# Block 2's attention with keys in token layout and queries turned by VectorE

## The chip, the core and the metric

The kernel runs on one core of a Trainium2 chip. A core has five engines that each work through a queue of their own in order: TensorE (PE in the profile; its weight loads are listed apart as PEld), VectorE (DVE), ScalarE (ACT), GpSimd (POOL) and SyncE (SP), whose queue here issues nearly all DMA transfers. An instruction that waits for a semaphore holds up everything behind it on its own engine. The metric is the device time of one execution in microseconds (us); lower is better.

## What is computed

```python
# q, k, v: (8 batches, 8 heads, 576 tokens, 64) f32
q_s = exp(q - max(q, axis=-1));  q_s = q_s / (sum(q_s, axis=-1) + 1e-9)   # over the 64 of a head
k_s = exp(k - max(k, axis=2));   k_s = k_s / (sum(k_s, axis=2) + 1e-9)    # over the 576 tokens
kv  = einsum('bhsd,bhse->bhde', k_s, v)                                   # 64x64 per head
x   = einsum('bhsd,bhde->bhse', q_s, kv)       # then heads side by side: 4608 tokens x 512
h   = x @ w_in                                 # 512 -> 2048, weights given in float64
g   = h * clip(h + 3, 0, 6) / 6
out = g @ w_out                                # 2048 -> 512
```

## The kernel before

The 4608 tokens are worked off in six pieces: blocks 0, 1 and 2 of 512 tokens each, by a plain matrix product, and then three large blocks of 1024 tokens each, by a product with seven instead of eight sub-products (functions `factors`, `phase1`, `phase2`). The attention of a piece is made while the piece ahead of it is multiplied. So block 2's attention, which the change rewrites, is made in the loop `j == 1`, beside block 1's matrix products, and the first large block's attention in the loop `j == 2`.

Loop j goes over 16 chunks of 128 hidden units; I call them f0 to f15. In a chunk TensorE does 12 matmuls `ph <- x, w` (the first product, `gemm1`), ScalarE and VectorE make `g` from `ph` (`relu6`) and split it into two parts `gp` (a ScalarE cast, then a VectorE subtraction on line 121), and TensorE does 12 matmuls `po <- w, gp` (the second product, `gemm2`). The second product of a chunk comes behind the first product of the next one (`pend`, one chunk of lag). Both parts of every operand are used, three matmuls for one product, to keep float32 accuracy. Beside this each chunk of block 1 makes sums of weights for the large blocks (`sum_weights`: VectorE additions `v <- w` and `v <- v`, splits `gp <- v`, and DMA stores `wf <- gp`). Tile `gp` has four buffers, which the splits of `g` and of the sums share.

The attention of a block is four units, one for each pair of heads (`hp`). Each unit is a generator, and `steps` advances it by a step or two per chunk. A unit of block 2 before, `attention(2, hp)`, runs so:

- loads `kt` (keys with channels on the partitions, 128x576), `qt` (queries with tokens on the partitions, 128x512) and `vt` (values);
- `km`, a VectorE maximum over `kt`, then a ScalarE exponential of `kt`; `q_softmax` with `lean`: a VectorE maximum `qm`, eight ScalarE exponentials that also give the sums `qr`, then VectorE normalizes `qt`;
- on TensorE, five turnings of `kt` into tiles `pe` and `pe2` and four of `qt` into `tp` (`flip`, line 93), which ScalarE copies to `ke` (keys with tokens on the partitions) and `qT`;
- ten pairs of small matmuls `pkv <- vt, ke`, whose result VectorE scales to `kv`; the matmuls `px <- qT, kv`; and a split of `px` into block 2's `x`.

A unit of a large block, `sb_attention(s, hp)`, goes another way: it loads the keys twice, `kt` for the maximum only and `ke` in token layout; the maximum is spread by GpSimd to a 128x128 tile `kb`, which TensorE turns with one flip into `pm`; VectorE subtracts it from `ke`, and ScalarE takes the exponential. Its queries come in a layout `qf` in which every 32x32 block is already standing the wrong way, so that VectorE's own 32x32 transposes give `qT` (in tile `m`). A head's 64 channels then lie on two groups of 32 partitions, so the maximum and the sum have to be combined across partitions: `both_halves` lets GpSimd copy 32 partitions at a time into `swap`, and VectorE combines (line 304).

What sets the order: a scheduler places the instructions of VectorE, ScalarE, GpSimd and SP at build time. On TensorE, from block 1 on, the order is that of the program (`keep_in_program_order`). `kt` and `qt` have one buffer each, `ke` and `vt` two, `km` and `kb` two.

Of the kernel before, what the change touches and what calls it, by code (L numbers as in the profile page):

```python
# [18 lines left out]
P = 128  # L19
# [13 lines left out]
def attention_moe(  # L33
# [51 lines left out]
    def mm(out, lhsT, rhs, start, stop, goes_on=False):  # L85
        ordered(
            nc.tensor.matmul(  # L87
                out, lhsT, rhs, start=start, stop=stop, skip_group_check=goes_on
            )
        )  # L90
# [199 lines left out]

    NG = SB // QD
    START = NB * TB

    def across(t):
        return t.rearrange("p (g o) -> p g o", o=1).broadcast_to([P, NG, QD])

    def both_halves(stat, op):
        swap = att.tile([P, NG], F32, name="swap", bufs=2)  # L300
        for r in range(0, P, QD):
            o = r ^ QD
            nc.gpsimd.tensor_copy(swap[r : r + QD], stat[o : o + QD])  # L303
        nc.vector.tensor_tensor(stat, stat, swap, op=op)

    def q_softmax_t(qt):
        qs = qt.rearrange("p (g d) -> p g d", d=QD)
        qm = att.tile([P, NG], F32, name="qm", bufs=2)
        qr = att.tile([P, NG], F32, name="qr", bufs=2)
# [4 lines left out]
        nc.vector.tensor_reduce(qr, qs, axis=AX.X, op=ALU.add)  # L314
# [4 lines left out]
        qT = moe.tile([P, 2 * DM], F32, name="m", bufs=1)[:, 0:SB]  # L319
        nc.vector.transpose(qT, qt)  # L320
        return qT

# [2 lines left out]
    def x_of(s):  # L325

        if "x" not in held:
            held["x"] = xp.tile([P, NCC, SB], F32, name="x32", tag="xa")
        return held["x"]

    def sb_attention(s, hp):
        t0 = START + s * SB
        need = [b for b in range(t0 // S, (t0 + SB - 1) // S + 1)]
        qt = att.tile([P, SB], F32, name="qt", bufs=1)
        nc.sync.dma_start(qt, qf[s, hp])
        loads = {b: load_k(b, hp, tokens=True) for b in need if (b, hp) not in kvs}
        yield
        new = {}
        for b, (kt, ke, vt) in loads.items():
            km = att.tile([P, 1], F32, name="km", bufs=2)  # L340
            nc.vector.tensor_reduce(km, kt, axis=AX.X, op=ALU.max)
            kb = att.tile([P, P], F32, name="kb", bufs=2)
            nc.gpsimd.tensor_copy(kb, km.broadcast_to([P, P]))
            new[b] = ke, vt, kb
        qT = q_softmax_t(qt)
        yield
        for ke, vt, kb in new.values():
            pm = bank_a("pm")
            flip(pm[:, 0:P], kb)
            nc.vector.tensor_sub(  # L350
                ke, ke, pm[:, 0:P].rearrange("p (o n) -> p o n", o=1).broadcast_to([P, NCH, P])
            )
            nc.scalar.activation(ke, ke, AF.Exp)
        yield
        yield
        for b, (ke, vt, kb) in new.items():
            kv_of(b, hp, ke, vt)
        yield
        x = x_of(s)
        for c in range(2):  # L360
            px = bank_a("px")
            at = t0 + c * TH
            for b in need:
                lo, hi = max(b * S - at, 0), min((b + 1) * S - at, TH)
                if lo < hi:
                    sl = slice(c * TH + lo, c * TH + hi)
                    mm(px[:, lo:hi], kvs[b, hp], qT[:, sl], True, True)
            nc.scalar.copy(x[:, hp, c * TH : (c + 1) * TH], px[:, 0:TH])
        yield


    A11, A12, A22, S1, S2, S3, S4 = range(7)
# [333 lines left out]
    def steps(units, length):  # L706
        before = None
        for unit in units:
            next(unit)
            yield  # L710
            if before:
                next(before, None)
            for _ in range(length - 2):
                next(unit)
                yield
            before = unit
        yield
        next(before, None)
        yield
# [19 lines left out]
    for j in range(NB):  # L739
        if j == 1:  # L740
            in_order.append(True)
        if j < NB - 1:
            step = steps([attention(j + 1, hp) for hp in range(NP)], 4)
        else:
            step = steps([sb_attention(0, hp) for hp in (0, 2, 1, 3)], 6)
            fac = factors(0)
        chunks = [*range(NFC)] if j < NB - 1 else [NFC - 1, *range(NFC - 1)]
        for n, f in enumerate(chunks):
            if not j and f + AHEAD < NFC:
                load_w(f + AHEAD)  # L750
            g = gemm1(j, f)
            if not j and f + 2 < NFC:
                decode(f + 2)
            if j == 1 and f % 2:
                plain_weights(f // 2, 0)
                plain_weights(f // 2, 1)
            if j:
# [19 lines left out]

    for s in range(NS):
        more = s + 1 < NS
        step = steps([sb_attention(s + 1, hp) for hp in (0, 2, 1, 3)], 6) if more else iter(())  # L780
# [12 lines left out]
        phase1(s, between1)  # L793
        phase2(s, between2)
        for _ in fac:
            pass
# [5 lines left out]
def _laid_out(q, k, v, moe_w_in, moe_w_out):  # L802
# [4 lines left out]
    n_first = _OUTS[0][0][0]  # L807
# [10 lines left out]
    if w.dtype != np.float64:  # L818
# [1 line left out]
    return {  # L820
        "q": tokens.transpose(0, 3, 2, 1, 4, 5),
        "qf": rows[n_first:]
        .reshape(-1, SB // QD, QD, NP, 4, QD)
        .transpose(0, 3, 4, 2, 1, 5)
        .reshape(-1, NP, P, SB),
        "kT": k.transpose(0, 1, 3, 2).reshape(B, NP, 2 * D, S),
        "k": by_chunk(np.pad(k, pad, constant_values=LOWEST)),
        "v": by_chunk(np.pad(np.concatenate([v, ones], axis=-1), pad)),
# [31 lines left out]
```

## Time and profile before

| | |
|---|---|
| median of 3 runs | 872.07 us (871.47 to 872.77) |
| the profiled execution | 867.29 us, of which the span is 865.5 us |
| granted TensorE clock, mean | 0.988 |
| PE busy | 819.9 us, 95% of the span |
| DVE busy | 674.1 us, 78% |
| ACT busy | 459.1 us, 53% |
| POOL busy | 68.2 us, 8% |
| DMA | 190.99 MB, 221 GB/s over the span |

The busy times are sums over the whole span; what an engine does in one stage is read from a window of the trace. In a row of the trace's timeline the first number is the start in us from the span's start, the second how long the piece took, then engine, source line, operation, tiles (written `<-` read), shape, and how many instructions were merged; in square brackets, the idle time of the engine ahead of it and what ended that. On VectorE the end of one instruction overlaps the start of the next, so what an instruction costs its queue is the distance from start to start, a little less than its own duration.

### The profile page before, as it was taken

What the parts mean: (1) busy time and instruction counts of PE and PEld (TensorE: products, weight loads), DVE (VectorE), ACT (ScalarE), POOL (GpSimd) and SP (SyncE); (2) the same over time, 40 slices, a digit from 0 to 9 for tenths busy, and PEclk for the clock granted to TensorE, in tenths of its full rate; (3) what the DMA queues carried; (4) which work ended last, traced back from release to release, by engine and by line L of the source; (5) the groups of instructions that cost most, each with busy time, mean ns of one, the idle gap of its engine ahead of it and who ended that gap; (6) DMA issues with size and microseconds to landing.
All of it is one profiled execution on the core that took longest, in us unless ns stands there. A gap on an engine that the chain in (4) does not pass through costs nothing.

```text
span 865.5 us, 11820 instructions
## 1 busy us (share of the span) xinstructions
PE 819.9 (95%) x4064; PEld 657.5 (76%) x4064; DVE 674.1 (78%) x1064; ACT 459.1 (53%) x789; POOL 68.2 (8%) x142
## 2 busy tenths in 40 slices
PE   5789998899999998999998999999999999999997
PEld 4568776677887876888786787777788788887886
DVE  7998997885957889579988986588597846648763
ACT  7887665554434445355555553554555634444543
POOL 5111211000100110101102000011000000000000
PEclk9889999999999999999999999999999999999999
DMA  9997654675639661488775566765556775555572
GB/s 368 413 409 265 219 181 161 210 258 201 226 139 316 223 228 58 135 286 266 267 261 176 190 219 226 240 223 172 164 179 195 228 237 194 195 193 191 193 234 87
DMA packets 73531, 190.99 MB, mean 221 GB/s; under 512 B 7168, under 2 KB 19456, under 8 KB 71424
## 3 DMA queue, kind: packets, MB, share of 16 engines
q1 hardware_dynamic: 72896, 189.20, 63.8%
q10 hardware_dynamic: 576, 1.05, 0.3%
q8 instruction: 32, 0.52, 0.3%
q14 instruction: 27, 0.22, 0.1%
HBM read 146.18 MB, written 44.04 MB: 220 GB/s over the span
## 4 chain that ended last, share of the span: by engine, by line
PE 60%; DVE 16%; DMA 5%; issue 4%; ACT 3%; POOL 1%; ACTq 0%; DVEq 0%; SPq 0%; POOLq 0%
PE x L87 25%; PE y L87 10%; PE z L87 9%; PE po L87 7%; PE ph L87 6%; DVE g L498 2%; DVE gp L121 1%; DMA kt<-in_kT_dram 1%; PE px L87 1%; DMA wf<-gp 1%; PE pkv L87 1%; ACT qt L221 1%; DMA out_dram<-v 1%; DMA v<-whole 1%; POOL swap L303 1%
## 5 line engine op out<-in xcount | busy, mean ns | idle before, releaser
L120 ACT CAST gf<-g 128x512 fp32r<-128x512 f32 x168 | 104.2, 624 | 96.4 <-DVE gf L121 48.6
L87 PE MATMUL po<-w,gp 128*128 128x512 f32 x576 | 145.1, 400 | 5.3 <-DVE gp L121 4.3
L87 PE MATMUL ph<-x,w 128*128 128x512 f32 x576 | 144.9, 399 | 2.7 <-POOL w L121 1.3
L121 DVE TENSOR_TENSOR gf<-g,gf 128x512 fp32r<-128x512 f32 x168 | 113.3, 689 | 31.7 <-ACT gf L120 31.0
L87 PEld LDWEIGHTS ph<-x,w 128*128 128x128 f32 x576 | 109.8, 192 | 28.6 <-POOL w L121 1.7
L87 PEld LDWEIGHTS po<-w,gp 128*128 128x128 f32 x576 | 107.3, 190 | 30.2 <-DVE gp L121 5.4
L87 PE MATMUL x<-right,gp 128*128 128x512 f32 x384 | 95.0, 392 | 2.8 <-DVE g L538 2.8
L87 PE MATMUL x<-gf,gp 128*128 128x512 f32 x384 | 89.0, 389 | 0.0
L87 PEld LDWEIGHTS x<-right,gp 128*128 128x128 f32 x384 | 71.6, 188 | 19.1 <-DVE g L538 3.6
L87 PEld LDWEIGHTS x<-gf,gp 128*128 128x128 f32 x384 | 72.1, 188 | 15.0
L497 ACT ACTIVATE g<-ph,three 128x512 f32<-128x512 f32 x48 | 33.0, 691 | 67.7 <-PE ph L87 67.7
L497 ACT ACTIVATE v<-g,three 128x1024 f32<-128x1024 f32 x24 | 27.7, 1154 | 39.6 <-DVE g L542 39.6
L87 PE MATMUL x<-right,left 128*128 128x512 f32 x192 | 47.8, 392 | 0.8 <-DVE g L538 0.8
L87 PE MATMUL y<-right,gp 128*128 128x512 f32 x192 | 48.2, 395 | 0.0
L120 ACT CAST gp<-g 128x512 fp32r<-128x512 f32 x48 | 29.8, 622 | 33.4 <-DVE g L498 30.7
L87 PE MATMUL z<-gf,gp 128*128 128x512 f32 x192 | 45.8, 392 | 0.9 <-DVE gf L121 0.8
L87 PE MATMUL x<-gf,left 128*128 128x512 f32 x192 | 45.9, 392 | 0.8 <-DVE gf L121 0.7
L498 DVE SCALAR_TENSOR_TENSOR g<-g,ph 128x512 f32<-128x512 f32 x48 | 32.4, 677 | 15.4 <-ACT g L497 15.3
L87 PEld LDWEIGHTS z<-gf,gp 128*128 128x128 f32 x192 | 35.7, 188 | 10.0 <-DVE gf L121 2.6
L87 PEld LDWEIGHTS x<-gf,left 128*128 128x128 f32 x192 | 35.7, 188 | 9.7 <-DVE gf L121 2.5
L87 PEld LDWEIGHTS x<-right,left 128*128 128x128 f32 x192 | 35.7, 188 | 8.6 <-DVE g L538 1.3
L87 PEld LDWEIGHTS y<-right,gp 128*128 128x128 f32 x192 | 35.6, 188 | 8.0 <-issue 0.5
(135 smaller groups left out, 1323.3 us busy)
## 6 DMA issues: line engine op xcount, KB each, us to landing
gp<-wf SPq DMA_DIRECT2D x112, 512.0 KB, 3.4
left<-wf SPq DMA_DIRECT2D x56, 512.0 KB, 3.5
raw<-in_w_dram SPq DMA_DIRECT2D x16, 1024.0 KB, 14.2
wf<-gp SPq DMA_DIRECT2D x64, 256.0 KB, 2.6
wf<-w SPq DMA_DIRECT2D x48, 256.0 KB, 4.1
vt<-in_v_dram SPq DMA_DIRECT2D x28, 325.0 KB, 5.5
kt<-in_kT_dram SPq DMA_DIRECT2D x28, 288.0 KB, 3.5
ke<-in_k_dram SPq DMA_DIRECT2D x20, 320.0 KB, 4.9
```

The costliest lines, as they stand in the source:

```text
L87: nc.tensor.matmul(out, lhsT, rhs, start=start, stop=stop, skip_group_check=goes_on)
L120: nc.scalar.copy(hi, src)
L121: engine.tensor_sub(lo, src, hi.bitcast(F32))
L221: nc.scalar.activation(qs[:, i], qs[:, i], AF.Exp, bias=qm[:, i : i + 1], accum_out=qr[:, i : i + 1],)
L303: nc.gpsimd.tensor_copy(swap[r : r + QD], stat[o : o + QD])
L497: nc.scalar.activation(r, h, AF.Relu, bias=three, scale=1.0)
L498: nc.vector.scalar_tensor_tensor(g, r, 6.0, h, op0=ALU.min, op1=ALU.mult)
```

## The change

Block 2's four units are made as the large blocks' units are: `sb_attention` becomes a general `token_attention(t0, n, hp, put)` over n tokens, and block 2 uses it with n = 512 through `block_attention`. The array `qf` now also holds block 2's queries, in pieces of 512 tokens; a large block loads two pieces in one transfer. The helpers of the softmax take their width from the tile they are given. `put` says what is done with `px`: a split for block 2, a copy for a large block. A unit now has six steps instead of four, and in the loop `j == 1` two steps instead of one are taken in each chunk.

```diff
+    TURNED = 2 * TB
...
-    def sb_attention(s, hp):
-        t0 = START + s * SB
-        need = [b for b in range(t0 // S, (t0 + SB - 1) // S + 1)]
-        qt = att.tile([P, SB], F32, name="qt", bufs=1)
-        nc.sync.dma_start(qt, qf[s, hp])
+    def token_attention(t0, n, hp, put):
+        need = [b for b in range(t0 // S, (t0 + n - 1) // S + 1)]
+        qt = att.tile([P, SB], F32, name="qt", bufs=1)[:, 0:n]
+        at = (t0 - TURNED) // TB
+        nc.sync.dma_start(
+            qt.rearrange("p (b n) -> p b n", n=TB),
+            qf[at : at + n // TB, hp].rearrange("b p n -> p b n"),
+        )
         loads = {b: load_k(b, hp, tokens=True) for b in need if (b, hp) not in kvs}
         yield
...
-        x = x_of(s)
-        for c in range(2):
+        for c in range(n // TB):
             px = bank_a("px")
-            at = t0 + c * TH
+            at = t0 + c * TB
...
+            put(c, hp, px)
+        yield
+
+    def sb_attention(s):
+        def put(c, hp, px):
+            nc.scalar.copy(x_of(s)[:, hp, c * TB : (c + 1) * TB], px)
+        return [token_attention(START + s * SB, SB, hp, put) for hp in (0, 2, 1, 3)]
+
+    def block_attention(j):
+        def put(c, hp, px):
+            x_hi, x_lo = x_block(j)
+            split(x_hi[:, hp, :], x_lo[:, hp, :], px)
+        return [token_attention(j * TB, TB, hp, put) for hp in range(NP)]
...
         if j < NB - 1:
-            step = steps([attention(j + 1, hp) for hp in range(NP)], 4)
+   X * TB >= TURNED          # TURNED = 2 * TB
+            units = block_attention(j + 1) if turned else [attention(j + 1, hp) for hp in range(NP)]
+            step = steps(units, 6 if turned else 4)
...
-            for _ in range((2 if f % 4 == 3 else 1) if j < 2 else 2 if n < 14 else 1):
+            for _ in range((2 if f % 4 == 3 else 1) if not j else 2 if n < 14 else 1):
                 next(step, None)
```

On TensorE, in the second and third chunk of block 1 (`w_334` is the weight tile of f1, `w_366` that of f2, `w_306` that of f0), the order changes so:

```order
 L87 MATMUL po<-w_1165,gp 128x512 x12
 L87 MATMUL ph<-x_564,w_334 128x512 x12
-L93 MATMUL pe<-ident,kt 128x128 x4
-L93 MATMUL pe_1383<-ident,kt 64x128
-L93 MATMUL tp<-ident,qt 128x128 x4
+L93 MATMUL pm<-ident,kb 128x128
 L87 MATMUL po<-w_306,gp 128x512 x12
 L87 MATMUL ph<-x_564,w_366 128x512 x12
```

The nine flips of a unit are gone, and one stands in their place; this happens four times in block 1's products.

On VectorE, at the change from block 0 to block 1, before (`gp_1196` and `gp_1227` are the splits of block 0's last two chunks, `x1_564` is block 1's x, `g_1255` is f0's g):

```order
L233 TENSOR_SCALAR qr_1290<-qr_1290 128x8
L234 RECIPROCAL qr_1290<-qr_1290 128x8
L235 TENSOR_TENSOR qt_1284<-qt_1284,qr_1290 128x512
L121 TENSOR_TENSOR gp_1196<-g_1193,gp_1196 128x512
L498 SCALAR_TENSOR_TENSOR g_1224<-g_1224,ph_1211 128x512
L121 TENSOR_TENSOR gp_1227<-g_1224,gp_1227 128x512
L121 TENSOR_TENSOR x1_564<-px_1077,x1_564 128x512
L498 SCALAR_TENSOR_TENSOR g_1255<-g_1255,ph_1242 128x512
```

And the same place now (`km_1535`, `km_1699` and `km_1877` are the key maxima of units 1, 2 and 3):

```order
L121 TENSOR_TENSOR gp_1196<-g_1193,gp_1196 128x512
L305 TENSOR_TENSOR qm_1291<-qm_1291,swap_1294 128x16
L347 TENSOR_REDUCE km_1535<-kt_1468 128x1
L314 TENSOR_TENSOR qt_1279<-qt_1279,qm_1291 128x512
L515 SCALAR_TENSOR_TENSOR g_1224<-g_1224,ph_1211 128x512
L316 TENSOR_REDUCE qr_1292<-qt_1279 128x16
L347 TENSOR_REDUCE km_1699<-kt_1688 128x1
L121 TENSOR_TENSOR gp_1227<-g_1224,gp_1227 128x512
L305 TENSOR_TENSOR qr_1292<-qr_1292,swap_1303 128x16
L121 TENSOR_TENSOR x1_564<-px_1077,x1_564 128x512
```

Ahead of the split of block 1's x now stand a subtraction, a sum and two key maxima that were not there, and the normalization of `qt` has moved behind it; the third maximum and the transposes stand between that split and f0's g.

On SP's queue at the same place, now (`kt_1688` and `kt_1833` are the keys of units 2 and 3, `kt_2271` the first large block's; before, the three stores of `w_15` were followed at once by the stores of `gp_1269`):

```order
L147 DMA whole_89<-v_1160 128x1024
L283 DMA kt_1468<-in_kT_dram 128x576
L416 DMA wf0_90<-w_15_1165 128x2x256
L416 DMA wf1_91<-w_15_1165 128x2x256 x2
L283 DMA kt_1688<-in_kT_dram 128x576
L283 DMA kt_1833<-in_kT_dram 128x576
L283 DMA kt_2271<-in_kT_dram 128x576
L338 DMA qt_1466<-in_qf_dram 128x512
L405 DMA wf0_90<-gp_1269 128x512 x2
```

Four loads of keys into the one `kt` buffer now follow each other there, each of which has to wait until the maximum over the one before it has been taken.

More of the change, by code (lines that the diff above doesn't have):

```diff
@@ L289, in load_k @@
         return kt, ke, vt
-    NG = SB // QD
     START = NB * TB
+    TURNED = 2 * TB
     def across(t):
-        return t.rearrange("p (g o) -> p g o", o=1).broadcast_to([P, NG, QD])
+        return t.rearrange("p (g o) -> p g o", o=1).broadcast_to([P, t.shape[1], QD])
     def both_halves(stat, op):
-        swap = att.tile([P, NG], F32, name="swap", bufs=2)
+        n = stat.shape[1]
+        swap = att.tile([P, SB // QD], F32, name="swap", bufs=2)[:, 0:n]
         for r in range(0, P, QD):
@@ L306, in q_softmax_t @@
     def q_softmax_t(qt):
+        n = qt.shape[1]
         qs = qt.rearrange("p (g d) -> p g d", d=QD)
-        qm = att.tile([P, NG], F32, name="qm", bufs=2)
-        qr = att.tile([P, NG], F32, name="qr", bufs=2)
+        qm = att.tile([P, SB // QD], F32, name="qm", bufs=2)[:, 0 : n // QD]
+        qr = att.tile([P, SB // QD], F32, name="qr", bufs=2)[:, 0 : n // QD]
         nc.vector.tensor_reduce(qm, qs, axis=AX.X, op=ALU.max)
@@ L318, in q_softmax_t @@
         nc.vector.tensor_mul(qs, qs, across(qr))
-        qT = moe.tile([P, 2 * DM], F32, name="m", bufs=1)[:, 0:SB]
+        qT = moe.tile([P, 2 * DM], F32, name="m", bufs=1)[:, 0:n]
         nc.vector.transpose(qT, qt)
@@ L358, in sb_attention @@
         yield
-        x = x_of(s)
-        for c in range(2):
+        for c in range(n // TB):
             px = bank_a("px")
-            at = t0 + c * TH
+            at = t0 + c * TB
             for b in need:
-                lo, hi = max(b * S - at, 0), min((b + 1) * S - at, TH)
+                lo, hi = max(b * S - at, 0), min((b + 1) * S - at, TB)
                 if lo < hi:
-                    sl = slice(c * TH + lo, c * TH + hi)
-                    mm(px[:, lo:hi], kvs[b, hp], qT[:, sl], True, True)
-            nc.scalar.copy(x[:, hp, c * TH : (c + 1) * TH], px[:, 0:TH])
+                    mm(px[:, lo:hi], kvs[b, hp], qT[:, c * TB + lo : c * TB + hi], True, True)
+            put(c, hp, px)
         yield
+    def sb_attention(s):
[7 more added lines that the diff above has]
+        return [token_attention(j * TB, TB, hp, put) for hp in range(NP)]
     A11, A12, A22, S1, S2, S3, S4 = range(7)
@@ L742, in attention_moe @@
         if j < NB - 1:
-            step = steps([attention(j + 1, hp) for hp in range(NP)], 4)
+            turned = (j + 1) * TB >= TURNED
+            units = block_attention(j + 1) if turned else [attention(j + 1, hp) for hp in range(NP)]
+            step = steps(units, 6 if turned else 4)
         else:
-            step = steps([sb_attention(0, hp) for hp in (0, 2, 1, 3)], 6)
+            step = steps(sb_attention(0), 6)
             fac = factors(0)
@@ L779, in attention_moe @@
         more = s + 1 < NS
-        step = steps([sb_attention(s + 1, hp) for hp in (0, 2, 1, 3)], 6) if more else iter(())
+        step = steps(sb_attention(s + 1), 6) if more else iter(())
         fac = factors(s + 1) if more else iter(())
@@ L806, in _laid_out @@
     rows = q.transpose(0, 2, 1, 3).reshape(B * S, NP, 2 * D)
-    n_first = _OUTS[0][0][0]
+    n_first = 2 * TB
     tokens = rows[:n_first].reshape(n_first // TB, NC4, P, NP, 2, D)
@@ L822, in _laid_out @@
         "qf": rows[n_first:]
-        .reshape(-1, SB // QD, QD, NP, 4, QD)
+        .reshape(-1, TB // QD, QD, NP, 4, QD)
         .transpose(0, 3, 4, 2, 1, 5)
-        .reshape(-1, NP, P, SB),
+        .reshape(-1, NP, P, TB),
         "kT": k.transpose(0, 1, 3, 2).reshape(B, NP, 2 * D, S),
```

## The prediction

> **What bounds the kernel now.** I read the busy times of the page first, then the same in windows of the trace, then TensorE's timeline in block 1, and last who waits for whom on VectorE there.
>
> ```profile
> PE 819.9 (95%) x4064; PEld 657.5 (76%) x4064; DVE 674.1 (78%) x1064; ACT 459.1 (53%) x789; POOL 68.2 (8%) x142
> ```
>
> TensorE is busy for 95% of the span, so time is to be had only where its own path gets shorter, or where it waits. Block 1's products reach from the end of f0's first product (145.66) to the end of f15's (247.9). The windows below give, after the length, busy us (and instructions) of PE, PEld, DVE, ACT and POOL, the granted clock, the share of the DMA engines and GB/s.
>
> ```profile
> 145.66:247.90 102.24, 97.61 (x505) 78.41 (x504) 77.46 (x154) 50.52 (x121) 4.75 (x18) 1.00 0.60 205
> ...
> 158.00:170.00 12.00, 11.09 (x67) 8.59 (x65) 11.93 (x30) 8.40 (x27) 0.00 (x0) 1.00 0.44 157
> 170.00:182.00 12.00, 11.07 (x66) 8.87 (x67) 11.83 (x28) 7.80 (x26) 0.00 (x0) 1.00 0.64 224
> ...
> 140.00:150.00 10.00, 9.00 (x37) 6.67 (x36) 6.37 (x12) 5.82 (x13) 0.00 (x0) 1.00 0.00 0
> 270.00:280.00 10.00, 8.11 (x38) 6.43 (x37) 8.03 (x15) 4.18 (x8) 0.59 (x2) 1.00 1.02 393
> ```
>
> In this stage TensorE sets the pace, at a full clock. But VectorE has no free time from 158 to 182 (11.93 and 11.83 us of 12), although it has 24.8 us over the whole stage (102.24 less 77.46). These two facts decide the case: the change takes work from TensorE and ScalarE, and gives some to VectorE.
>
> **What is removed from TensorE.** A unit's nine flips stand in the program's order between a `ph` (or `px`) and the next `po`, and two of their steps wait until ScalarE has emptied a bank.
>
> ```profile
> 153.69 0.71 PE L93 MATMUL pe<-ident,kt 128*128 128x128 f32 x5
> ...
> 155.52 2.98 PE L87 MATMUL po<-w,gp 128*128 128x512 f32 x12
> ...
> 168.49 0.60 PE L93 MATMUL pe<-ident,kt 128*128 128x128 f32 x4
> 170.05 0.30 PE L93 MATMUL pe<-ident,kt 128*64 128x128 f32 x1 [0.95 <-ACT ke L246]
> ...
> 171.61 3.01 PE L87 MATMUL po<-w,gp 128*128 128x512 f32 x12
> ...
> 190.04 0.60 PE L93 MATMUL pe<-ident,kt 128*128 128x128 f32 x4
> ...
> 192.45 2.98 PE L87 MATMUL po<-w,gp 128*128 128x512 f32 x12
> ...
> 205.43 0.60 PE L93 MATMUL pe<-ident,kt 128*128 128x128 f32 x4
> ...
> 207.72 2.98 PE L87 MATMUL po<-w,gp 128*128 128x512 f32 x12
> ...
> 258.79 0.38 PE L93 MATMUL pm<-ident,kb 128*128 128x128 f32 x2
> 258.92 3.02 PE L87 MATMUL po<-w,gp 128*128 128x512 f32 x12
> ```
>
> From a unit's first flip to the `po` behind it pass 1.83, 3.12, 2.41 and 2.29 us, together 9.65. Now one flip `pm` stands there. The large blocks show its price: two of them hold the `po` up by 0.13 us, so four cost some 0.3. The `pkv` and `px` matmuls stay the same in number and size. **Term A: 9.65 less 0.3 is 9.3 us off TensorE's path**, if it waits for nothing new.
>
> **What is added to VectorE.** Per unit: `qt` minus its maximum, a second maximum-like reduction for the sum, two small combinations with `swap`, the subtraction of `pm` from `ke`, and the transpose. Rows for these, the groups from 140 to 330 us (busy, mean ns, idle before); the last two show the distance from start to start.
>
> ```profile
> L219 DVE TENSOR_REDUCE qm<-qt 128x8 f32<-128x512 f32 x3 | 2.0, 682 | 0.0
> L320 DVE STREAM_TRANSPOSE m<-qt 128x1024 f32<-128x1024 f32 x4 | 5.0, 1243 | 0.3 <-PE px L87 0.3
> L350 DVE TENSOR_TENSOR ke<-ke,pm 128x640 f32<-128x640 f32 x8 | 6.3, 812 | 0.6 <-PE pm L93 0.6
> L304 DVE TENSOR_TENSOR qm<-qm,swap 128x32 f32<-128x32 f32 x5 | 0.9, 184 | 1.2 <-POOL swap L303 1.2
> ...
> 170.44 0.69 DVE L235 TENSOR_TENSOR qt<-qt,qr 128x512 f32<-128x512 f32 x1
> 171.04 0.69 DVE L121 TENSOR_TENSOR x<-px,x 128x512 fp32r<-128x512 f32 x1
> ```
>
> An instruction costs the queue 0.09 us less than its duration (0.60 for 0.69). So a unit adds 0.60 for the subtraction, 0.59 for the sum, 0.58 for the transpose (half of 1243 ns, less 0.09 at most), 0.72 for `ke`, and twice 0.1: 2.7 us, in four units 10.8. The maximum over `kt`, the one over `qt` and the normalization are there before and after. VectorE's 77.46 us become 88.3, in a stage that would last 102.24 less 9.3, so 92.9. It would be 95% busy, with 4.6 us to spare instead of 24.8.
>
> **What ScalarE gives up.** Eight exponentials with their sums become one. The first starts at 177.97, and the next thing behind the eighth at 180.64, 2.67 us later:
>
> ```profile
> 177.97 0.34 ACT L221 ACTIVATE qt<-qt,qm 128x64 f32<-128x64 f32 x1
> ...
> 180.64 0.61 ACT L120 CAST gp<-g 128x512 fp32r<-128x512 f32 x1
> ```
>
> The cast of `gp` that waits there stands on the way to the next `po`, so this shortens the way from `ph` to `gp`. ScalarE does not bound the stage (50.52 of 102.24 us), so I count nothing for it beyond what helps VectorE to keep up.
>
> **The change to block 1.** In the new order the split of block 1's x, for which TensorE waits, has a subtraction, a sum and two key maxima ahead of it, and the second of these needs keys whose load can only be issued when the maximum ahead has been taken. The rows: the split, TensorE behind it, three maxima that waited for their keys, and how long a load of `kt` takes.
>
> ```profile
> 140.56 0.17 DVE L233 TENSOR_SCALAR qr<-qr 128x8 f32<-128x8 f32 x1 [1.27 <-ACT qt L221]
> ...
> 144.19 0.68 DVE L121 TENSOR_TENSOR x<-px,x 128x512 fp32r<-128x512 f32 x1
> ...
> 144.93 0.73 PE L87 MATMUL ph<-x,w 128*128 128x512 f32 x2 [0.33 <-DVE x L121]
> ...
> 157.51 0.75 DVE L238 TENSOR_REDUCE km<-kt 128x1 f32<-128x576 f32 x1 [0.92 <-DMA kt<-in_kT_dram]
> ...
> 195.87 0.75 DVE L238 TENSOR_REDUCE km<-kt 128x1 f32<-128x576 f32 x1 [2.01 <-DMA kt<-in_kT_dram]
> ...
> 211.99 0.75 DVE L341 TENSOR_REDUCE km<-kt 128x1 f32<-128x576 f32 x1 [3.96 <-DMA kt<-in_kT_dram]
> ...
> DMA to landing us min/median/max: 2.7/3.1/4.9
> ```
>
> Added ahead of it are 0.60, 0.59 and two maxima of 0.66 (0.75 less 0.09), 2.5 us; gone are the normalization and two small ones (0.9), and the wait of 1.27 for the eight exponentials. That leaves 0.3. A load of `kt` lands 2.7 to 4.9 us after its issue, and VectorE has only about 1.8 us of other work between these two maxima, so it stands for 0.9 to 3.1 us more, of which up to 0.9 falls into a wait that it had anyway for a cast of ScalarE. **Term B: 0.8 us lost**, with 0 and 2.5 as its bounds; I take a value near the lower one, since the DMA engines are idle from 140 to 150 (share 0.00). The next key load, of unit 3, holds VectorE again before f0's g; behind it TensorE still has two `po` groups, 5.4 us, so I count nothing; without that cover it would be another 2 us.
>
> **Term C: VectorE late in the first chunks.** I went through its new order from f0 to f7 with the distances above. f1's g now has behind the stores of block 0's result a maximum that waits for unit 1's queries, a sum and a `ke` subtraction ahead of it, and between f1's g and its `gp` a key maximum and two 0.60 additions. It comes some 1.5 us after TensorE would want it; f3's `gp`, behind a transpose, a `ke` subtraction and a maximum over freshly loaded queries, is late by 1.4 more, and f5 and f6 by some 0.5. From f1's g to f7's VectorE has 37 instructions of 0.60 (22.2), 23 additions of 0.33 (7.6), three maxima of 0.66, two transposes, two `ke` and small ones (6.3 together), 36.1 us, and TensorE six fifteenths of 92.9, 37.2 us, so a delay isn't made up there; from f8 on it is, since its load falls to some 4.5 us for a chunk of 5.4. The nearest stage in which VectorE is full and the same kind of unit runs is the next one, with these waits:
>
> ```profile
> 275.91 0.30 PE L93 MATMUL pm<-ident,kb 128*128 128x128 f32 x1 [1.89 <-ACT x L368]
> ...
> 312.39 0.30 PE L93 MATMUL pm<-ident,kb 128*128 128x128 f32 x1 [1.00 <-DVE ke L350]
> ```
>
> They sum to 2.9 us over four units with more VectorE work each. **I take 3.5 us**, which is near that row's sum; the bounds are 0 (the lag of one chunk covers all) and the whole of A (VectorE sets the pace).
>
> **What costs nothing.** Four loads of `ke`, 320 KB each, 1.3 MB, come to a stage whose DMA engines are 60% busy at 205 GB/s. Were they full, as from 270 to 280 at 393 GB/s, it would be 3.3 us. The queries in two pieces instead of one are the same bytes. GpSimd gets 32 `swap` copies and four `kb`, on an engine that is busy for 4.75 us of 102. On SP's queue the stores of `gp_1269` now stand behind key loads and a load of queries that waits for unit 0's transpose. By the same count that is at about 150; before they were issued here:
>
> ```profile
> 149.19 1.80 SPq L388 DMA_DIRECT2D wf<-gp  x4
> ```
>
> **The sum**, against the profiled execution: 867.29 - 9.3 + 0.8 + 3.5 = 862.3 us, so 5.0 us less. That execution was 4.8 us below the median of the runs, 872.07, so on the runs' scale I forecast 867.1.
>
> **The rivals.**
>
> *All of A is kept.* The lag of one chunk and the shorter way through ScalarE hide C: 872.07 - 9.3 + 0.8 is 863.6 us. For it: in the stretch from 158 to 182 VectorE was full already, and no `po` waited for `gp` there. Against it: that VectorE has 4.6 us to spare where it had 24.8.
>
> *Slower: VectorE stands at the key maxima.* `kt` has one buffer, and eight maxima (four of block 2, four of the first large block) stand in VectorE's queue between block 0's last chunk and f9, each ahead of a g or a `gp`. Three that had to wait before are among the rows shown with term B. With their mean of 2.3 us eight make 18.4, and 88.3 + 18.4 is 106.7 us for the stage, 4.5 more than now: 876.5. It decides from 13.9 us of idle VectorE on (102.24 less 88.3). Against it: only the first maxima follow each other closely; the later loads are issued some 10 us ahead. The Trainium skill, Perfetto Trace Analysis, Optimizing Scalar/DVE Operations, advises moving work from a saturated DVE to Scalar; this change moves it the other way. The rows from 158 to 182 bear out that VectorE is saturated for that part of the stage, not for all of it.
>
> *GpSimd's copies block VectorE.* 36 of 0.21 us would add 7.5 us to 88.3, 95.8 in place of 92.9, and the loss C would be some 3 us larger: 870. One row looks like it, a subtraction of 0.69 us that took 2.82 while GpSimd made a wide subtraction of its own; the copies are a smaller matter (the last row gives their shortest, median and longest in ns):
>
> ```profile
> 134.29 2.82 DVE L121 TENSOR_TENSOR gp<-g,gp 128x512 fp32r<-128x512 f32 x1
> ...
> 221.57 1.51 POOL L303 COPY swap<-qr 32x32 f32<-32x32 f32 x4 [4.92 <-DVE qr L314]
> 222.02 0.41 DVE L416 TENSOR_TENSOR v<-v 128x256 f32<-128x256 f32 x1
> 222.35 0.42 DVE L418 TENSOR_TENSOR v<-v 128x256 f32<-128x256 f32 x1
> ...
> L303 POOL COPY swap<-qm x20: 199/207/573, 214.6 to 324.0; 32x32 f32<-32x32 f32 x20
> ```
>
> While four copies ran, VectorE additions of 256 columns took 0.41 and 0.42 us and followed each other by 0.33. The Trainium skill, SBUF — State Buffer, SBUF: two separate sides, calls the shared port pair "an exclusive lock, not a bandwidth split", held for a whole instruction; by that rule this rival would be the likely one. The trace agrees for the wide subtraction and not for these copies.
>
> *Given back in the next stage.* From 270 to 280 the DMA engines are full and TensorE is busy for 8.11 of 10 us. If those loads could not start earlier, about all of the gain would go there: 872. Against it: they are issued when units advance, which comes earlier as well.
>
> **How the numbers follow.** My forecast (864.8 to 869.5) has 0.48, all of A 0.22, the key maxima 0.14, the next stage 0.10, GpSimd 0.06. The range from 862.8 to 872.5 leaves out the key maxima and a little at the lower end. About 0.2%, 1.7 us, is what a measurement of this kernel can tell from no change. Below 870.3 lie the forecast, all of A, and part of GpSimd: 0.75. Within 0.2%: the next stage and the rest, 0.12. Above 873.8: 0.13.
>
> **What would show it.** Right: between `ph` and `po` of block 1 a `pm` with a gap of 0.1 to 0.2 us, f0 to f15 in 95 to 98 us instead of 102.24, waits of `po` for the VectorE `gp` that sum to 2 to 5 us between f1 and f7, VectorE some 11 us and ScalarE some 14 us busier and less busy in all, and block 2 and the large blocks as long as before. Wrong: waits of VectorE for `kt` of over 10 us in that stage, or a first large block that starts no earlier.

## The result and the profile after

The changed kernel takes 863.15 us (median of 6 runs, 860.57 to 864.14), the kernel before beside it 871.5 (median of 6, 869.78 to 872.77). The ratio is 0.9903, interval 0.9888 to 0.9919: 8.35 us or 1.0% faster. In a second group of runs it was 861.77 against 869.69, ratio 0.9911 (0.9892 to 0.9931). The forecast was 867.1 us, 5.0 less than the 872.07 of before; the rival nearest to the result is "all of A is kept" (863.6).

The profiled execution took 863.42 us, its span 861.6. First the page's busy times, then one stretch of each kernel, from block 1's first `po` to f15's `ph` (columns as in the prediction):

```profile
PE 816.8 (95%) x4032; PEld 654.0 (76%) x4032; DVE 683.7 (79%) x1088; ACT 443.6 (51%) x717; POOL 80.1 (9%) x178
```

```profile
145.50:245.18 99.68, 95.05 (x493) 76.31 (x492) 77.12 (x154) 50.52 (x121) 4.75 (x18) 1.00 0.61 209
```

```profile
146.47:239.84 93.37, 92.15 (x462) 73.93 (x460) 80.86 (x165) 39.00 (x64) 11.95 (x40) 0.98 0.66 222
```

The first of the two is before, the second after. The stretch is 6.3 us shorter, and TensorE stands idle for 1.2 us of it instead of 4.6. VectorE is busy for 80.86 of 93.37 us, ScalarE for 11.5 us less. By the prediction's own marks f0 to f15 is 102.24 less 6.3, 95.9 us, within the 95 to 98 named. Over the span VectorE has 9.6 us more (forecast 11), ScalarE 15.5 less (forecast 14).

TensorE's timeline of after, at the places that the prediction named:

```profile
145.89 0.74 PE L87 MATMUL ph<-x,w 128*128 128x512 f32 x2 [1.31 <-DVE x L121]
146.47 7.23 PE L87 MATMUL po<-w,gp 128*128 128x512 f32 x24
...
156.26 0.27 PE L93 MATMUL pm<-ident,kb 128*128 128x128 f32 x1
156.29 3.00 PE L87 MATMUL po<-w,gp 128*128 128x512 f32 x12
...
169.28 0.27 PE L93 MATMUL pm<-ident,kb 128*128 128x128 f32 x1
169.31 3.01 PE L87 MATMUL po<-w,gp 128*128 128x512 f32 x12
...
214.35 1.14 PE L87 MATMUL px<-m,kv 128*128 128x128 f32 x4 [1.22 <-DVE m L322]
```

`pm` holds the next `po` up by 0.03 us where the nine flips took 1.83 to 3.12. No `po` of block 1 waits for `gp` in this profile. Two waits are new or longer: 1.31 us for the split of block 1's x, and 1.22 us for unit 3's transpose. And the 24 `po` matmuls behind the first of them took 7.23 us: these have half a clock for a while, as the windows further below show.

All profiles of this study are compared by four marks on TensorE: the first `po` behind block 1's x, the first `pm` beside block 2's products (a flip for the first large block), the first product of the large blocks, the end of the span (us, differences of starts in each profile):

| kernel | to `po` | `po` to `pm` | `pm` to large | large to end | span | median of runs, ratio to before (interval) |
|---|---|---|---|---|---|---|
| before | 145.50 | 113.29 | 106.01 | 500.70 | 865.5 | 871.5 |
| before, second | 145.78 | 113.95 | 105.95 | 501.22 | 866.9 | 869.70, 1.0002 (0.9987 to 1.0018) |
| changed | 146.47 | 106.97 | 105.61 | 502.55 | 861.6 | 863.15, 0.9903 (0.9888 to 0.9919) |
| changed, second | 147.10 | 107.32 | 104.31 | 501.57 | 860.3 | 861.77, 0.9911 (0.9892 to 0.9931) |
| old unit, new pace | 146.15 | 112.94 | 107.59 | 501.42 | 868.1 | 871.45, 1.0022 (1.0004 to 1.0040) |
| keys only | 146.29 | 112.86 | 106.03 | 502.12 | 867.3 | 870.91, 1.0010 (0.9997 to 1.0023) |
| queries only | 147.22 | 107.93 | 106.47 | 501.68 | 863.3 | 866.11, 0.9958 (0.9942 to 0.9975) |
| keys, `tp` later | 147.94 | 105.79 | 107.61 | 501.66 | 863.0 | 864.60, 0.9945 (0.9926 to 0.9965) |
| flips apart | 146.03 | 107.44 | 108.98 | 501.25 | 863.7 | 866.07, 0.9954 (0.9938 to 0.9970) |
| more VectorE | 147.05 | 114.73 | 105.29 | 501.93 | 869.0 | 872.47, 1.0033 (1.0018 to 1.0048) |
| x split first | 144.15 | 112.23 | 106.15 | 501.07 | 863.6 | 866.22, 0.9968 (0.9952 to 0.9983) |
| sums later | 146.96 | 103.84 | 104.68 | 502.52 | 858.0 | 859.81, 0.9879 (0.9854 to 0.9904) |
| sums later, x first | 144.08 | 106.59 | 104.15 | 501.98 | 856.8 | 859.27, 0.9872 (0.9847 to 0.9896) |
| before, sums later | 145.66 | 112.59 | 103.63 | 502.02 | 863.9 | 866.59, 0.9959 (0.9945 to 0.9974) |

### The profile page after: what moved, and what is told of

It is laid out like the page before. It is cut to its first block, busy times and chain, and to the rows that moved or that the text cites. A ratio compares the mean times of both kernels' runs of the same rounds, so it can differ in the third digit from the quotient of the medians.

```text
span 861.6 us, 11761 instructions
## 1 busy us (share of the span) xinstructions
PE 816.8 (95%) x4032; PEld 654.0 (76%) x4032; DVE 683.7 (79%) x1088; ACT 443.6 (51%) x717; POOL 80.1 (9%) x178
## 4 chain that ended last, share of the span: by engine, by line
PE 67%; DVE 18%; DMA 5%; issue 4%; ACT 3%; POOL 1%; SPq 0%; ACTq 0%; DVEq 0%; POOLq 0%
PE x L87 24%; PE po L87 12%; PE ph L87 10%; PE y L87 9%; PE z L87 9%; DMA kt<-in_kT_dram 2%; DVE g L515 2%; PE px L87 2%; PE pkv L87 2%; DVE gp L121 1%; DVE gf L121 1%; DVE v L141 1%; DVE right L121 1%; DVE km L347 1%; DMA wf<-gp 1%
## 5 line engine op out<-in xcount | busy, mean ns | idle before, releaser
L87 PE MATMUL ph<-x,w 128*128 128x512 f32 x576 | 147.9, 405 | 4.4 <-POOL w L121 2.0
L87 PE MATMUL po<-w,gp 128*128 128x512 f32 x576 | 146.9, 404 | 3.5 <-DVE gp L121 2.2
L87 PEld LDWEIGHTS ph<-x,w 128*128 128x128 f32 x576 | 111.7, 195 | 31.5 <-POOL w L121 2.9
L514 ACT ACTIVATE g<-g,three 128x512 f32<-128x512 f32 x24 | 17.4, 725 | 39.5 <-DVE g L548 39.5
```

The costliest lines, as they stand in the source:

```text
L87: nc.tensor.matmul(out, lhsT, rhs, start=start, stop=stop, skip_group_check=goes_on)
L514: nc.scalar.activation(r, h, AF.Relu, bias=three, scale=1.0)
```

## The experiments

Each median stands beside runs of the kernel before, whose medians in the groups of runs were 869.94 (experiments 1 to 4), 869.69 (5, 6, 8 and 9), 870.38 (7, 10 and 11) and 870.41 (12). The diffs are shortened; a line that starts with `#` stands for code.

**1. The old unit at the new pace.** `attention(2, hp)` unchanged in what it computes, cut into the six steps of the new one:

```diff
+        kt, ke, vt = load_k(j, hp); qt = ...; nc.sync.dma_start(qt, q[j, hp])
+        yield                      # loads one step ahead
+        # km, exp(kt), q_softmax (eight exponentials)
+        yield
+        # pe, pe2, tp: nine flips
+        yield; yield
+        # kv; yield; px, split; yield
```

> Block 2's units as before (all nine flips, eight exponentials), but cut into six steps at two steps per chunk, with the loads one step ahead of their use, as the changed kernel has it. TensorE's order is the same as before except that two px groups come one chunk earlier. Theory 'flips' (the gain is the flips' time off TensorE's path): no change, -1.5 to +1.5 us against the kernel before; the gaps with flips in block 1 still sum to 8 to 10 us and f0 to f15 take 98 to 103 us. Rival 'pace' (the earlier loads and the earlier steps are what helped): -4 us or more, and f0 to f15 in under 97 us.

871.45 us, ratio 1.0022; `po` to `pm` 112.94 instead of 113.3 to 114.0. The pace brings nothing (by the medians it costs 1.5 us), so the gain lies in what the units do.

**2. Keys only, 3. queries only.** From here on the pace is the same, and one half of the change is made at a time.

Against the old unit at the new pace, keys only has:

```diff
-        kt, ke, vt = load_k(j, hp)
+        kt, ke, vt = load_k(j, hp, tokens=True)
...
-        nc.scalar.activation(kt, kt, AF.Exp, bias=km)
+        nc.gpsimd.tensor_copy(kb, km.broadcast_to([P, P]))
         q_softmax(qt, True, nc.vector)
...
-        # five flips of kt into pe and pe2, copied to ke
+        flip(pm[:, 0:P], kb)
+        nc.vector.tensor_sub(ke, ke, pm[:, 0:P]...broadcast_to([P, NCH, P]))
+        nc.scalar.activation(ke, ke, AF.Exp)
         # four flips of qt into tp, copied to qT
```

and queries only:

```diff
-        nc.sync.dma_start(qt, q[j, hp])
+        nc.sync.dma_start(qt, qf[0, hp])
...
-        q_softmax(qt, True, nc.vector)
+        qT = q_softmax_t(qt)
...
         # five flips of kt into pe and pe2, copied to ke
-        # four flips of qt into tp, copied to qT
```

> Pace as in the changed kernel; only the keys go the new way (loaded in token layout, maximum by GpSimd and one flip pm); the queries keep four flips and eight ScalarE exponentials. Theory 'flips': a gap of a unit is now one pm and four tp flips without an emptied bank between, some 0.75 us instead of 2.4, so 4 x 1.65 = 6.6 us less; -5 to -7.5 us against before. Rival 'ScalarE relief' (the eight exponentials that became one brought the gain, since the cast of gp waited behind them): -3 us or less, since these exponentials are all still here. Rival 'VectorE nearly paces': more gain than the changed kernel, -9 us or more, because VectorE has only the ke subtraction more (2.9 us in all instead of 10.8).

> Pace as in the changed kernel; only the queries go the new way (one exponential, GpSimd's swap copies, VectorE's transposes); the keys keep five flips with the emptied bank between. Theory 'flips': four tp flips and the wait ahead of them gone, some 0.9 us a unit, so 3.6; -2 to -4.5 us against before, and with keys_only it adds up to about the whole gain (8.35). Rival 'ScalarE relief': -6 us or more, nearly the whole gain, since the exponentials go here. Rival 'VectorE nearly paces': 0 or slower, since 7.8 of the 10.8 us on VectorE come with the queries.

Keys only gained nothing (870.91), queries only 3.8 us (866.11), both together 8. Theory 'flips' had queries only right and missed keys only; 'ScalarE relief' allowed for keys only and missed queries only; 'VectorE nearly paces' missed both. The trace of keys only shows why. TensorE's timeline behind block 1's x and at unit 1, then VectorE's at unit 1:

```profile
146.29 6.73 PE L87 MATMUL po<-w,gp 128*128 128x512 f32 x24
...
169.05 0.27 PE L93 MATMUL pm<-ident,kb 128*128 128x128 f32 x1
171.67 0.63 PE L93 MATMUL tp<-ident,qt 128*128 128x128 f32 x4 [2.35 <-issue]
172.05 4.58 PE L87 MATMUL po<-w,gp 128*128 128x512 f32 x12
```

```profile
170.76 0.81 DVE L395 TENSOR_TENSOR ke<-ke,pm 128x640 f32<-128x640 f32 x1
```

Only one flip stands ahead of `tp` now, yet `tp` starts 2.6 us behind it, 0.1 us after VectorE ends the subtraction that reads `pm` (170.76 + 0.81 = 171.57). Tiles `pkv`, `px`, `pm` and `tp` share two banks. The row of `tp` names nothing that it waited for; by these times it was the bank of `pm`, which came free late because VectorE had other work ahead of the subtraction. At unit 3 it is the same (1.84 us, 0.1 us behind that subtraction; the row names a ScalarE cast, which had ended 0.5 us earlier). And the 12 `po` behind it took 4.58 us instead of 2.98, at half a clock: a wait of 2.35 us cost 3.9. Over the four units the time from the first flip to the `po` behind it is 6.4 us instead of 9.65, so 3.2 were won; the half clock here and behind block 1's x (24 `po` in 6.73 us instead of 5.61) took 2.7 of them back. In queries only the `pe2` flip still waits 1.24 and 0.73 us for a bank.

**4. Before, a second profile.** The same kernel.

> The kernel before, unchanged, for a second profile of it and a time beside it. Its profiled execution here took 867.3 us where its timed runs take about 871.5. If that profile was a lucky one because it missed half-clock windows of TensorE, this one should show one or two more windows of 3.4 us at half clock, between 100 and 150 us or elsewhere, and a span of about 869 to 870 us; if the profile is always shorter than the timed runs, it shows 865 to 866 again with the same clock.

Its span was 866.9: one more half-clock window than in the first profile, at 105 us (ten `ph` took 4.12 us instead of 2.56), but not the 869 to 870 that I expected. What the windows do shows in the runs: the 78 runs of this kernel beside the experiments reach from 866.7 to 874.3 us, and on the whole their mean time is the lower the higher the mean granted clock: 872.05 at 0.979 (3 runs), 870.7 at 0.984 (15), 868.4 at 0.988 (11). The execution I summed against (0.988, 867.3) was from the quick end.

**5. The changed kernel, a second profile.** The same kernel.

> The changed kernel, unchanged, beside the kernels of this group, for a second profile of it. Against before: -7 to -8.5 us. If the two half-clock windows of its first profile (at about 106 and 147 us of the span, some 1.6 us each) follow from the waits ahead of them, they are there again; if such a wait only sometimes makes a window, one or both are missing and the span is 1.6 or 3.2 us shorter.

861.77 us, 7.9 less than before. The wait for x was longer than in the first profile, 2.03 us, and no half-clock window followed. Nor did one follow a wait of 1.28 us at 105 us, where the first profile has 1.30 and ten `ph` in 4.13 us instead of 2.56. Rows of the windows from 145 to 150 us and of TensorE's timeline, first profile and then second:

```profile
145.00:150.00 5.00, 4.11 (x12) 3.31 (x13) 3.91 (x10) 1.45 (x3) 0.00 (x0) 0.72 0.37 105
```

```profile
145.00:150.00 5.00, 3.47 (x15) 2.91 (x16) 4.44 (x10) 0.83 (x2) 0.00 (x0) 1.00 0.29 71
```

```profile
146.53 0.73 PE L87 MATMUL ph<-x,w 128*128 128x512 f32 x2 [2.03 <-DVE x L121]
147.10 5.61 PE L87 MATMUL po<-w,gp 128*128 128x512 f32 x24
```

The clock is 0.72 in the one and 1.00 in the other, and the same 24 matmuls take 7.23 and 5.61. So a wait of 1 to 2 us may be followed by a half-clock window that costs 1.6 us more, or not, in the same kernel; the last section shows on what it depends. In the second profile another wait came, which the first has not (VectorE, then TensorE):

```profile
195.64 0.42 DVE L433 TENSOR_TENSOR v<-v 128x256 f32<-128x256 f32 x1 [3.67 <-DMA v<-whole]
```

```profile
197.66 1.20 PE L87 MATMUL po<-w,gp 128*128 128x512 f32 x4 [2.23 <-DVE gp L121]
```

VectorE stood 3.67 us for a load of weights for the sums, with a `gp` queued behind it.

**6. The keys' half with its query flips one step later.** The same work as keys only; `tp` no longer stands behind `px` and `pm` in units 1 and 3.

```diff
         nc.scalar.activation(ke, ke, AF.Exp)
+        yield
         tp = bank_a("tp")
...
         nc.scalar.copy(qT, tp)
-        yield
         yield
```

> keys_only with the four query flips of a unit one step later, so that in units 1 and 3 they no longer stand right behind px and pm in TensorE's queue. The number of flips on TensorE and all work of VectorE and ScalarE stay as in keys_only. Theory 'a bank's wait' (keys_only gained nothing since tp waited 2.35 and 1.84 us for a bank that VectorE freed late, and a half-clock window of 1.6 us followed): -5 to -8 us against keys_only, no wait at tp over 0.3 us. Theory 'flips' as I had it (what counts is the flips taken away): no change against keys_only, -1 to +1 us.

864.60 us, 6.3 less than keys only and 5.1 less than before. TensorE has no wait left from `po` to f15, with 16 flips of queries still there and eight exponentials per unit on ScalarE. At unit 1:

```profile
169.60 0.27 PE L93 MATMUL pm<-ident,kb 128*128 128x128 f32 x1
169.63 3.01 PE L87 MATMUL po<-w,gp 128*128 128x512 f32 x12
...
175.20 0.60 PE L93 MATMUL tp<-ident,qt 128*128 128x128 f32 x4
```

That settles two points: ScalarE's relief is not what the gain in block 1 comes from, and it is the place of the flips in TensorE's queue that counts, not only their number. Its `po` to `pm` is even shorter than the changed kernel's (105.79), since it has none of the waits and half-clock windows that the changed kernel's two profiles show in this stretch; part of that went again in block 2 (107.61).

**7. All nine flips, spread apart.** Block 2's unit as before, no work added to VectorE; the flips `pe` in one chunk, `pe2` and `tp` in the next, the kv matmuls in the one after, and two steps in every chunk of block 1.

```diff
+        # four flips pe -> ke
+        yield; yield
+        # flip pe2 -> ke, four flips tp -> qT
+        yield; yield
+        # kv ...
-            step = steps(units, 6 if turned else 4)
+            step = steps(units, 8 if turned else 4)
```

> Block 2's units as before, all nine flips on TensorE, eight exponentials, no added work on VectorE; only spread over eight steps so that in each unit the four flips pe, the flip pe2 with the four tp, and the kv matmuls stand in three different chunks, and no flip stands right behind the one whose bank it needs. Theory 'waits' (what the change saves is waits for a bank inside TensorE's queue, not the flips' own time): gaps of some 0.4 and 0.4 us per unit instead of 2.4, so 4 x 1.6 = 6.4 us off the stage; -4.5 to -7 us against before. Theory 'flips' as I predicted it (the nine flips had to go): -2 to +1 us against before.

866.07 us, 4.3 less than before. Unit 0 on TensorE:

```profile
154.22 0.60 PE L93 MATMUL pe<-ident,kt 128*128 128x128 f32 x4
154.57 2.99 PE L87 MATMUL po<-w,gp 128*128 128x512 f32 x12
...
160.13 0.27 PE L93 MATMUL pe<-ident,kt 128*64 128x128 f32 x1
160.24 0.60 PE L93 MATMUL tp<-ident,qt 128*128 128x128 f32 x4
160.59 3.01 PE L87 MATMUL po<-w,gp 128*128 128x512 f32 x12
```

The gaps are 0.35 and 0.46, 0.81 a unit and 3.2 in four, where the same 36 flips took 9.65. So 6.4 of the 9.65 us were waits and what hangs on them, and 3.2 the flips themselves. `po` to `pm` is 107.44, about as short as the changed kernel's (106.97 and 107.32). But 3 us of it went again in block 2 (108.98 instead of about 106), where the first wait for a bank is now longer (3.22 us instead of 1.89) and a half-clock window follows, which before has not (0.83 granted from 270 to 275 and from 275 to 280):

```profile
271.92 0.30 PE L93 MATMUL pm<-ident,kb 128*128 128x128 f32 x1 [3.22 <-ACT x L377]
```

**8. More VectorE work.** Each transpose of block 2 done five times.

```diff
-        nc.vector.transpose(qT, qt)
+        for _ in range(5 if n == TB else 1):
+            nc.vector.transpose(qT, qt)
```

> The changed kernel with each of block 2's four transposes done five times (the same result written again), 4 x 0.62 = 2.5 us more on VectorE per unit, 9.9 us in all, nearly the added 10.8 us once more. Term C as predicted (VectorE nearly paces, TensorE waits for late gp): +4 to +9 us against the changed kernel, with waits of po for VectorE's gp that sum to 3 us or more. Rival 'the lag of one chunk hides it': 0 to +2 us.

872.47 us, 10.7 more than the changed kernel, beyond the 4 to 9 us of the one theory and far from the 0 to 2 of the other. From 165 to 185 us VectorE has no free time, and TensorE waits once for long (VectorE's window, then TensorE):

```profile
165.00:185.00 20.00, 15.56 (x85) 12.12 (x83) 20.00 (x43) 8.97 (x15) 1.52 (x5) 1.00 0.62 215
```

```profile
189.45 2.08 PE L87 MATMUL px<-m,kv 128*128 128x128 f32 x4 [8.89 <-DVE m L323]
```

It is `px` of unit 1 that waits, not `po`, and behind this wait TensorE runs at half clock (`px` takes 2.08 us instead of 1.03). So nearly all of the 10.7 us is lost at one place. Part of these 8.89 us is that `px` needs the last of the five transposes, so the run shows that the lag doesn't hide more VectorE work in this place, not how much slack there is elsewhere.

**9. Block 1's x split first.** The key maxima and the softmax of block 2's units queued on VectorE behind that split.

```diff
+        with tc.issue_after(held["behind"]) if n == TB else nullcontext():
             for b, (kt, ke, vt) in loads.items():
...
             qT = q_softmax_t(qt)
```

> The changed kernel with the key maxima and the query softmax of block 2's units queued on VectorE behind the last split of block 1's x. Theory 'term B' (TensorE waits 1.31 us for that split because maxima and softmax stand ahead of it, and the wait is followed by 3.4 us at half clock, which costs 1.6 us more): -1 to -3 us against the changed kernel, the wait under 0.4 us and no half-clock window from 145 to 152 us. Rival 'only moved' (VectorE is full after 158 us, and what is queued later there comes late for gp): 0 to +1.5 us against the changed kernel, with new waits of po for gp in f1 to f7.

866.22 us, 4.5 more than the changed kernel, beyond what either theory said. The first part came true: the wait for x is gone, and `po` starts at 144.15, 2.3 to 3.0 us earlier. It was lost again, and more, at one place, unit 1 (TensorE, then VectorE):

```profile
183.98 2.08 PE L87 MATMUL px<-m,kv 128*128 128x128 f32 x4 [5.01 <-DVE m L326]
```

```profile
183.23 0.70 DVE L326 STREAM_TRANSPOSE m<-qt 128x512 f32<-128x512 f32 x1
```

Pushed back, unit 1's softmax queued behind the additions and splits of the sums, and its transpose came at 183.23, when `px` had been due at 179. Behind the wait of 5.01 us TensorE ran at half clock again (`px` in 2.08 us instead of 1.03, the 12 `po` in 4.40 instead of 3.19).

**10. Sums later, 11. both, 12. the same in the kernel before.** No sums of weights are advanced in f1 to f5 of block 1.

```diff
-            if j:
+            if j == 2 or j and not 1 <= n <= 5:
                 next(sums, None)
```

> The changed kernel; in block 1's chunks f1 to f5 no sums of weights are advanced, so that five of the 26 steps of them (some 3.7 us of VectorE each) come after f5, where VectorE has room. Theory 'VectorE is full from 158 to 185 us' (term C's cause is right): the waits of px for m and of po for gp in block 1 (together 1.2 and 2.9 us in the two profiles of the changed kernel) are gone; -1 to -3 us against the changed kernel, so -9 to -11 us against before. Rival 'given back later': the sums come late in block 2 and the first large block waits for its weights; 0 to +3 us against the changed kernel.

> sums_later and x_split_first together. x_split_first lost 4.5 us against the changed kernel since px of unit 1 then waited 5.0 us for a transpose in the stretch where VectorE is full. If that stretch was the only reason, with the sums out of it the gain at the split of block 1's x is kept: -2 to -4 us against the changed kernel, no wait of px for m over 0.5 us. Rival 'unit 1 is late whatever else VectorE does' (its chain of GpSimd copies, exponential and transposes starts too late): px waits 3 us or more again, 0 to +4 us against the changed kernel.

> The kernel before with the one edit of sums_later (no sums of weights advanced in block 1's chunks f1 to f5), block 2's units as they were. If sums_later won 2.3 to 2.7 us against the changed kernel because the change's own VectorE work filled f1 to f6 (term C's cause), the kernel before, whose VectorE has room there and whose po waits nowhere for gp in block 1, gains little: -1 to +1 us. Rival 'the sums stood in the way anyway' (in block 1's flips, or in the next stage): -2 to -3 us, as much as the changed kernel won.

Sums later: 859.81 us, 10.6 less than the kernel before and 2.2 to 2.7 better than the changed kernel's difference. VectorE's load from 165 to 185 us, changed kernel and then this one:

```profile
165.00:185.00 20.00, 20.00 (x105) 16.02 (x104) 19.50 (x42) 8.35 (x15) 3.08 (x8) 1.00 0.75 239
```

```profile
165.00:185.00 20.00, 20.00 (x105) 15.98 (x105) 14.43 (x30) 6.47 (x10) 1.80 (x9) 1.00 0.26 81
```

TensorE has no wait from `po` to f15, and `po` to `pm` is 103.84, 3.1 and 3.5 less than in the two profiles of the changed kernel. With the x split first added (859.27) `px` of unit 1 no longer waits; `po` starts 2.9 us earlier than in sums later, and 2.8 of that goes between `po` and `pm` (1.3 in waits of `po` for `gp`, at 147.7, 222.3 and 228.2; the rest I have not placed). So the gain at the split of x was not kept. By the medians both are faster than the two kernels of this case, but the changed kernel did not run beside them, and the intervals of their ratios overlap with its intervals and with each other.

The kernel before gained 3.8 us by the same edit (866.59), more than I expected and against the first theory. But it gained elsewhere: `po` to `pm` fell by only 0.7 to 1.4 us, and 2.3 came in block 2. Part of that is a wait with a half-clock window behind it that is not there now (windows from 335 to 350 us, before and then before with sums later):

```profile
335.00:350.00 15.00, 12.48 (x47) 9.49 (x46) 12.05 (x15) 4.62 (x7) 0.00 (x0) 0.89 0.09 35
```

```profile
335.00:350.00 15.00, 13.65 (x61) 10.97 (x60) 15.00 (x20) 8.22 (x12) 0.00 (x0) 1.00 0.30 105
```

So the runs of 10 and 12 don't show that it was the change that had filled VectorE: in the kernel before it is busy for 19.18 of the 20 us from 165 to 185 as well. The gain in block 1, 3.1 and 3.5 us in the one and about 1 in the other, lies where that theory put it. But 1.6 of the 3.1 is the half-clock window of the first profile, and 2.2 of the 3.5 is the `po` behind a load for the sums in the second. The wait of `px` for a transpose, behind two splits of the sums in VectorE's queue, is 1.2 and 0.7 of it.

## Why the prediction was right, point by point

**Against the profiles** the sum was close: -5.0 us forecast, and the means of two spans each are 866.2 and 860.95, so -5.25. **Against the runs** it was too small, 5.0 for 8.35 and 7.9. The step that was off is the last one of the sum, "so on the runs' scale I forecast 867.1": it took the changed kernel's profiled execution to be 4.8 us quicker than the median of its runs, as the one of before was, and it was 0.3 slower (863.42 against 863.15). Why the two kernels differ by less in the profiles than in the runs is explained in part only: runs of before at the clocks of its two profiles took 868.4 (0.988) and 869.4 us (0.986) on average, about 1 us less than its usual run, and the rest of the 2.5 to 3 us stays open.

**Term A**, 9.3 us: right in size. The four gaps fell from 9.65 to 0.12, so 9.5. The words were too narrow: I called it the flips off TensorE's path. TensorE's waits in that stretch before add up to 4.7 us, in one row each for a kind (who waited for whom, us, times, longest), and after one is left:

```profile
PE pe L93 <- ACT ke L246: 2.4, 3, 1.0
PE tp L93 <- ACT ke L247: 1.3, 2, 0.9
PE tp L93 <- ACT ke L246: 0.7, 1, 0.7
PE tp L93 <- DVE x L121: 0.3, 1, 0.3
```

```profile
PE px L87 <- DVE m L322: 1.2, 1, 1.2
```

Flips apart took 6.4 of the 9.65 away with every flip in place.

**ScalarE** counted at nothing: right for block 1. Keys with `tp` later keeps all its exponentials and gains 5.1.

**Term B**, 0.8 us: `po` starts 0.97 later in the first profile and 1.3 in the second. The first profile of the changed kernel and the second of before have a half-clock window at 105 us in this, the other two have none; like against like it is 0.7 and 1.6. So the size was about right, and the cause is the one given:

```profile
143.80 0.75 DVE L347 TENSOR_REDUCE km<-kt 128x1 f32<-128x576 f32 x1 [0.75 <-DMA kt<-in_kT_dram]
...
145.15 0.69 DVE L121 TENSOR_TENSOR x<-px,x 128x512 fp32r<-128x512 f32 x1
```

The half-clock window behind it, 1.6 us in one profile of two, was not in the sum.

**Term C**, 3.5 us: the size was met, mostly by luck. From `po` to `pm` the two profiles are 6.3 and 6.6 us shorter, about 3 less than the gaps gave, but not by the way I gave. The premise was that VectorE would be 95% busy in this stage with 4.6 us to spare; it was busy for 80.86 of 93.37 us, with 12.5 to spare. Of the 10.8 us added, 3.7 showed in this stage (77.12 before); from 100 us to block 1's first `po` VectorE was busy for 2.3 us more and in block 2 for 5.7 more. f1's and f3's `gp` were not late. Part of the added work fell into time in which VectorE had stood waiting: the write behind the store of block 0's result, which had waited 3.6 us, waited 0.2 (before, then after):

```profile
DVE v L677 <- DMA out_dram<-v: 3.6, 1, 3.6
```

```profile
DVE v L694 <- DMA out_dram<-v: 0.2, 1, 0.2
```

What made up the 3 us instead was, in the first profile, the half-clock window behind the wait for x (1.6) and a transpose ahead of `px` (1.22), and in the second a `gp` behind a load (2.23) and the same transpose (0.69).

**What costs nothing**: the loads of `ke`, GpSimd's copies and the queries in two pieces, as said. One item that I had not priced: VectorE's waits for loads `v<-whole`, 0.4 us in block 1 before, are 4.0 and 4.9 after, and one of them reached TensorE in the second profile. **The rivals**: "all of A is kept" named 863.6, nearly the measured median, but not the way: of A's 9.3 us 6.3 to 6.6 were kept in block 1. VectorE stood at the key maxima for 1.1 us in the first profile, not 18. Nothing was given back in block 2, which was 0.3 to 1.7 us shorter (the 1.7 has one half-clock window fewer than before, from 335 to 350 us); the large blocks took 0.4 to 1.9 us longer, and I have not found why.

## What to carry to other kernels

In an in-order queue, price a group of instructions by what it waits for, and ask first whether the group can be spread out: with every flip kept, 6.4 of 9.65 us went by moving flips away from the one whose bank they needed. Two halves of a change that stand in one gap do not add up: the later wait sets it, so one half alone may bring nothing. Before work is moved to an engine with enough time on average, look at the stretch where it is full, and move something else out of there: the sums of weights, left out of five chunks and made later, brought about 2 us more by the medians, and 3.8 in the kernel before.

## What the runs showed of the hardware that I had not expected

A wait of TensorE of 1.3 to 2.4 us can cost 1.6 us more, since it is sometimes followed by 3.4 us at a granted clock of 0.50: 24 `po` in 7.23 instead of 5.61 us after a wait of 1.31, 12 in 4.58 instead of 2.98 after 2.35, but nothing after one of 2.03. Which of the two comes depends on where the wait falls. In each profile the half-clock windows start on one grid of 3.41 us (in the first of the changed kernel at 106.21, 147.17 and 338.32 us, 12 and 56 steps apart), which lies differently in each execution. What counts is TensorE's busy time in the step of the grid just ahead. Over the fourteen profiles, from 60 us on, a step with less than 45% was followed by half clock in 22 of 23 cases, one with 45 to 55% in 11 of 22, and one with more in none of 3200. The wait of 1.31 us, with one of 0.67 shortly ahead of it, fell into one step, busy for 52% of it; the one of 2.03 was split between two, busy for 63% (with 0.38 us added for a `px` matmul whose record is missing there) and 64%. The Trainium skill, TensorE: Matmul & The Clock Gate, What's actually happening, gives half rate after at least one idle window of about 3.4 us, in a window that runs freely. The traces agree with the length and with the free run; they differ on what counts as idle, for no wait of TensorE in those places lasted 3.4 us, and a step that was busy for up to about half of its time was enough.

Copies of 32 partitions on GpSimd did not hold VectorE up noticeably: with 12 us more of GpSimd's work VectorE's busy time rose by 9.6 us over the span, less than the 10.8 that the prediction counted from VectorE's own instructions.
